# Moving the load of one weight block (the z1 half of w_in) from SyncE's DMA queue to ScalarE's in the start-up of a fused gMLP and linear-attention kernel

## Chip, cores and metric

One core of one Trainium2 chip. Times are device microseconds (us) of one execution. A run of a kernel is profiled once and timed several times in turn with the kernel before on the same chip. Engines: PE is TensorE, PEld its weight loads, ACT ScalarE, DVE VectorE, POOL GpSimd, SP SyncE; "SPq" and "ACTq" are issues of DMAs by those two. All times of single events are counted from the start of the span.

## The reference, cut to what matters

```python
# x: 2048 x 512 (bf16).  F = 1376, Fh = 688
z  = gelu(x @ w_in)                       # w_in: 512 x 1376
z1 = z[:, :Fh]                            # block "z1" of w_in
z2 = layernorm(z[:, Fh:])                 # block "z2" of w_in
b  = (z1 * (w_sp @ z2 + b_sp[:, None])) @ w_out
a  = linear_attention(x, wqkv, w_phi) @ wo
g  = sigmoid((x * gate_w).sum(-1, keepdims=True))
out = g * a + (1 - g) * b
```

The change touches only how the z1 block of `w_in` (512 x 688, 688 KB) reaches the chip.

## The kernel before: the parts that the argument needs

```python
nc.sync.dma_start(out=xs[:, 0, :], in_=x2[0:P, :])           # x tiles 0 and 1, plain
nc.scalar.dma_start(out=xs[:, 1, :], in_=x2[P:2 * P, :])
load_z2w(nc.sync, 0); load_z2w(nc.scalar, 1); load_z2w(nc.sync, 2)   # z2 block by depth slice
nc.scalar.dma_start(out=gaterow[0:NDT, :], ...)
load_z2w(nc.scalar, 3)
# ... cut: first GELU table load on ScalarE
x_dma_T(2)                                # x tiles 2, 3: transposed by the DMA
x_dma_T(3)
for h in range(2):                        # the z1 block in two halves (L136)
    nc.sync.dma_start(
        out=w_z1[:, 2 * h:2 * h + 2, :], in_=w_in_v[:, 2 * h:2 * h + 2, 0:FH])
for i in range(4, 8):
    x_dma_T(i)
# ... cut: x tiles 8 to 15, bias, wqk (transposed), eight small w_phi loads, wv, w_sp (transposed)
```

PE and ACT keep the order in which the program is written. PE first transposes x tiles 0 and 1, then computes z2 for tiles 0 to 3, then z1 for tiles 0 to 3 (`z1_tile`: four depth slices, two matmuls each, so the fifth matmul is the first to read the second half), then z2 for tiles 4 to 7, and so on. ACT applies GELU to each tile as it takes it out of PSUM (the "evictions", L203 for z2, L257 for z1).

```python
for c in range(NCH):
    ts = list(range(c * 4, c * 4 + 4))
    for tt in ts:
        if c > 0:
            z2_tile(tt)
        # ... cut
    for tt in ts:
        z1_tile(tt)
        # ... cut
```

The softmax here doesn't subtract the row's maximum and nothing guards it: scores larger than these inputs give would overflow.

## Time and profile before

| | before |
|---|---|
| time, median of the first three runs | 206.46 us (206.36 to 206.66) |
| span of the profiled run | 204.29 us, its time 206.0 |
| PE busy | 98% |
| z1 half 0: issued, landed | 4.93, 8.84 |
| z1 half 1: issued, landed | 5.57, 9.91 |
| PE's gap before the fifth matmul of z1 tile 0 | 0.26 us |

How to read it: the chain of waits names what held PE up before 10 us; the timelines of SP and ACT show when the issues left. The timeline of ACT is a good gauge of PE's gaps: ACT's evictions follow PE at 1.17 us a tile, and a longer step is a gap on PE. The last z2 and the first z1 eviction of the kernel before (start, length, engine, line, what, in brackets ACT's idle time before it):

```profile
9.31 0.74 ACT L203 ACTIVATE z2all<-zp 128x688 bf16<-128x688 f32 x1 [0.43 <-PE zp L188]
10.74 0.74 ACT L257 ACTIVATE z1all<-zp 128x688 bf16<-128x688 f32 x1 [0.68 <-PE zp L188]
```

The step is 1.43, which is 0.26 above 1.17. The span minus 10.74 is 193.55 us; that number returns below.

### The profile page before, as it was taken

How to read it: one execution, taken by the hardware profiler on the slowest of the kernel's cores; microseconds unless marked ns; L12 is line 12 of the kernel's file. 1: busy time of each engine (PE TensorE's matmuls, PEld its weight loads, DVE VectorE, ACT ScalarE, POOL GpSimd, SP SyncE). 2: the span in 40 equal slices, each digit the busy share in tenths (PEclk: the TensorE clock that was granted, in tenths of full speed). 3: DMA queues.
4: the chain of work that ended last, by engine and by line, in shares of the span. 5: the costliest groups of instructions: out<-in, count | busy, mean ns of one | idle time of the engine just before them, and what ended most of it. 6: DMA issues, size and time to landing. Idle time of an engine off the chain costs nothing.

```text
span 204.3 us, 3996 instructions
## 1 busy us (share of the span) xinstructions
PE 200.5 (98%) x1557; PEld 119.7 (59%) x1557; DVE 130.4 (64%) x283; ACT 74.6 (37%) x122; POOL 45.6 (22%) x76
## 2 busy tenths in 40 slices
PE   8999999999999999999999999999999999999994
PEld 4666666655665555656565666555555555665642
DVE  4558484838977597979797789555566645633332
ACT  3556677795222333342424042222351136002303
POOL 3020202022523325424242442222204220200000
PEclk9999999999999999999999999999999999999999
DMA  6999399999999027941322229763667458552943
GB/s 200 232 176 153 65 207 232 219 290 231 259 240 232 3 39 158 311 94 21 70 52 41 51 39 115 141 130 59 110 160 80 90 114 183 64 96 51 139 81 104
DMA packets 89947, 27.22 MB, mean 133 GB/s; under 512 B 84200, under 2 KB 89928, under 8 KB 89928
## 3 DMA queue, kind: packets, MB, share of 16 engines
q1 hardware_dynamic: 87616, 24.81, 63.5%
q10 hardware_dynamic: 2312, 2.16, 3.8%
q8 instruction: 12, 0.20, 0.4%
q14 instruction: 7, 0.06, 0.1%
HBM read 4.15 MB, written 2.10 MB: 31 GB/s over the span
## 4 chain that ended last, share of the span: by engine, by line
PE 94%; DMA 4%; SPq 1%; DVE 0%; issue 0%
PE mm L451 37%; PE zp L188 16%; PE mm L352 14%; PE mm L512 9%; PE mm L506 7%; PE mm L392 7%; DMA w_z<-in_B_w_in_dram 2%; PE kvacc L408 2%; PE at L464 2%; DMA xs<-in_A_x_dram 1%; PE mm L517 1%; SPq L131 1%; PE zp L304 0%; SPq L136 0%; PE at L475 0%; PE pq L304 0%
## 5 line engine op out<-in xcount | busy, mean ns | idle before, releaser
L451 PE MATMUL mm<-z2all,wspT 128*128 128x344 bf16 x512 | 79.9, 309 | 0.0
L451 PEld LDWEIGHTS <-wspT 128*128 128x128 bf16 x512 | 49.0, 98 | 25.3
L188 PE MATMUL zp<-w_z,xT 128*128 128x344 bf16 (+1 forms) x254 | 38.1, 309 | 0.1
L356 ACT ACTIVATE eq<-mm 128x512 bf16<-128x512 f32 x32 | 17.4, 595 | 51.4 <-PE mm L352 25.7
L360 DVE TENSOR_REDUCE zs<-eq 128x64 f32<-128x1024 bf16 x16 | 19.5, 1220 | 20.1 <-ACT eq L356 20.1
L188 PEld LDWEIGHTS <-xT 128*128 128x128 bf16 x254 | 24.5, 98 | 12.1 <-issue 0.3
L356 ACT ACTIVATE ek<-mm 128x512 bf16<-128x512 f32 x32 | 17.3, 601 | 27.1 <-PE mm L352 27.1
L456 DVE SCALAR_TENSOR_TENSOR ucat<-mm,bT,z1all 128x344 bf16<-128x344 f32 x32 | 17.4, 544 | 15.1 <-PE mm L451 15.1
L369 POOL TENSOR_TENSOR eq<-eq,ratio 128x512 bf16<-128x512 bf16 x16 | 16.9, 1055 | 44.6 <-DVE ratio L368 36.7
L528 ACT ACTIVATE ob<-mm,g_inv 128x512 bf16<-128x512 f32 (+1 forms) x15 | 10.1, 680 | 33.1 <-PE mm L517 28.5
L360 DVE TENSOR_REDUCE zs<-ek 128x64 f32<-128x1024 bf16 x16 | 19.2, 1208 | 2.8 <-ACT ek L356 2.8
L512 PE MATMUL mm<-wspT,uT 128*128 128x512 bf16 (+2 forms) x85 | 20.1, 367 | 0.0
L352 PEld LDWEIGHTS <-xT 128*128 128x128 bf16 x128 | 12.2, 98 | 12.0
L369 POOL TENSOR_TENSOR ek<-ek,ratio 128x512 bf16<-128x512 bf16 x16 | 16.9, 1055 | 2.2 <-DVE ratio L368 1.7
L506 PE MATMUL mm<-wspT,oT 128*128 128x512 bf16 (+2 forms) x68 | 16.6, 366 | 0.0
L352 PE MATMUL mm<-wq_p,xT 128*128 128x512 bf16 x64 | 16.4, 379 | 0.0
L392 PE MATMUL mm<-wv_sb,xT 128*128 128x512 bf16 x64 | 16.4, 379 | 0.0
L352 PE MATMUL mm<-wk_p,xT 128*128 128x512 bf16 x64 | 16.3, 379 | 0.0
L206 DVE BATCH_NORM_STATS2 bn<-z2all 128x6 f32<-128x344 bf16 x32 | 14.9, 502 | 0.0
L203 ACT ACTIVATE z2all<-zp 128x688 bf16<-128x688 f32 x16 | 11.8, 743 | 7.1 <-PE zp L188 7.0
L257 ACT ACTIVATE z1all<-zp 128x688 bf16<-128x688 f32 x16 | 11.9, 743 | 5.3 <-PE zp L188 4.9
L512 PEld LDWEIGHTS <-uT 128*128 128x128 bf16 x85 | 8.1, 98 | 9.4 <-issue 0.2
(77 smaller groups left out, 142.0 us busy)
## 6 DMA issues: line engine op xcount, KB each, us to landing
out_dram<-ob ACTq DMA_DIRECT2D x12, 128.0 KB, 2.6
wspT<-in_B_w_out_dram SPq DMA_DIRECT2D x2, 640.0 KB, 5.2
w_z<-in_B_w_in_dram SPq DMA_DIRECT2D x2, 344.0 KB, 4.1
wv_sb<-in_A_wqkv_dram SPq DMA_DIRECT2D x1, 512.0 KB
wspT<-in_A_wo_dram SPq DMA_DIRECT2D x2, 256.0 KB, 4.1
out_dram<-ob SPq DMA_DIRECT2D x3, 128.0 KB, 1.8
w_z<-in_B_w_in_dram ACTq DMA_DIRECT2D x2, 172.0 KB, 3.3
w_z<-in_B_w_in_dram SPq DMA_DIRECT2D x2, 172.0 KB, 3.1
```

The costliest lines, as they stand in the source:

```text
L188: nc.tensor.matmul(zp[:, j, 0:n], lhsT=xT[:, dt, tt * P:(tt + 1) * P], rhs=wt[:, dt, j * HF:j * HF + n], start=(dt == 0), stop=(dt == NDT ...
L206: nc.vector.bn_stats(out=bn6[:, tt, j, :], in_=z2v[:, j, :])
L257: nc.scalar.activation(out=z1all[:, tt, :].rearrange("p (j n) -> p j n", j=2), in_=zp[:, :, 0:HF], func=AF.Gelu_apprx_tanh,)
L352: nc.tensor.matmul(ps[:, :], lhsT=xT[:, dt, tt * P:(tt + 1) * P], rhs=w[:, dt, :], start=(dt == 0), stop=(dt == NDT - 1))
L356: nc.scalar.activation(out=e[:, :, a, :], in_=ps[:, :].rearrange("p (h f) -> p h f", f=DH), func=AF.Exp, scale=1.0 - 2.0 * a)
L360: nc.vector.tensor_reduce(out=z[:].rearrange("p h a -> p (h a)"), in_=e[:].rearrange("p h a f -> p (h a) f"), axis=AX.X, op=ALU.add,)
L369: nc.gpsimd.tensor_tensor(out=e[:, :, 1, :], in0=e[:, :, 1, :], in1=ratio[:, :, None].to_broadcast([P, H, DH]), op=ALU.mult)
L392: nc.tensor.matmul(v_ps[:, :], lhsT=xT[:, dt, tt * P:(tt + 1) * P], rhs=wv_sb[:, dt, :], start=(dt == 0), stop=(dt == NDT - 1))
L451: nc.tensor.matmul(gp[:, 0:HF], lhsT=wspT[:, st, tt * P:(tt + 1) * P], rhs=z2all[:, st, j * HF:(j + 1) * HF], start=(st == 0), stop=(st == ...
L456: nc.vector.scalar_tensor_tensor(out=ucat[tt % NU][:, c0 + j * HF:c0 + (j + 1) * HF], in0=gp[:, 0:HF], scalar=bT[:, tt:tt + 1], in1=z1all[ ...
L506: nc.tensor.matmul(acc, lhsT=oTs[tt][:, g, :], rhs=wo_t[:, g, c0:c1], start=start and g == 0, stop=stop and g == NG - 1)
L512: nc.tensor.matmul(acc, lhsT=uTs[tt][:, i + ft, :], rhs=w_main[i][:, ft, c0:c1], start=start and ft == 0, stop=False)
```

## The change

Intent: ACT is idle between its copy of x tile 1 and its first eviction. If it issues the two z1 halves there, SP's queue holds transposed x tiles alone, these can be issued 1.1 us earlier, and the z1 block no longer stands behind x tiles 2 and 3.

```diff
-    for h in range(2):
-        nc.sync.dma_start(
-            out=w_z1[:, 2 * h:2 * h + 2, :], in_=w_in_v[:, 2 * h:2 * h + 2, 0:FH])
+    def load_z1w(eng, h):
+        eng.dma_start(out=w_z1[:, 2 * h:2 * h + 2, :], in_=w_in_v[:, 2 * h:2 * h + 2, 0:FH])
+
     for i in range(4, 8):
         x_dma_T(i)
@@
         x_T(1, 2, NDT, pq_tile([P, 2, P], BF16)[:, :, :], on_act=True)
+        for h in range(2):
+            load_z1w(nc.scalar, h)
         one(0, 0, 0)
```

## The prediction

> **What bounds the kernel now.** I read the page first (busy shares, slices, chain), then the chain in order of time over the first 30 us, then the timelines of SP and ACT there, the table by stretches, and last the waits each instruction carries in the program. The page says at once that TensorE is the bound:
>
> ```profile
> PE 200.5 (98%) x1557; PEld 119.7 (59%) x1557; DVE 130.4 (64%) x283; ACT 74.6 (37%) x122; POOL 45.6 (22%) x76
> PE   8999999999999999999999999999999999999994
> PEclk9999999999999999999999999999999999999999
> ```
>
> Between the start-up and the last output tiles PE is never idle and the granted clock is full. So any delay of PE before that is carried to the end one for one, and nothing after the start-up is there to be won. The change touches only the first 17 us. The chain in order of time there:
>
> ```profile
> 0.80 2.88 DMA xs<-in_A_x_dram
> ...
> 3.70 1.19 SPq L131
> ...
> 4.93 0.59 SPq L136
> ...
> 5.57 4.34 DMA w_z<-in_B_w_in_dram
> ...
> 9.96 13.59 PE zp L188 x92
> ```
>
> Columns are start, length, what. The second half of the z1 block is issued by SP at 5.57 and lands at 9.91, and from 9.96 PE runs without a pause: 13.59 / 92 = 148 ns per matmul. How long had PE waited? The timeline of PE and of its weight loads around it:
>
> ```profile
> 9.55 0.71 PE L188 MATMUL zp<-w_z,xT 128*128 128x344 bf16 x2
> 9.96 0.10 PEld L188 LDWEIGHTS <-xT 128*128 128x128 bf16 x1 [0.31 <-issue]
> ```
>
> The last matmul before the gap starts at 9.55, so the next was due at 9.55 + 0.148 = 9.70 and started at 9.96: a stall of 0.26 us. ScalarE shows the same, with z1 evictions 1.17 us apart but 1.43 us from the last z2 eviction to the first z1 one (9.31 to 10.74). This 0.26 us, 0.13% of the time, is all that an earlier z1 block can give. The matmul that stalls is the fifth of z1 tile 0, the first that reads the second half. The first was due at 9.55 - 3 x 0.148 = 9.11; the first half, issued at 4.93 with 3.9 us to landing, was there at 8.83.
>
> The issuing engines (timelines of SP and ACT):
>
> ```profile
> 2.20 2.69 SPq L131 DMA_TRANSPOSE xT<-in_A_x_dram  x2
> 4.93 1.10 SPq L136 DMA_DIRECT2D w_z<-in_B_w_in_dram  x2
> 6.08 5.13 SPq L131 DMA_TRANSPOSE xT<-in_A_x_dram  x4
> ...
> 4.47 0.37 ACT L280 COPY xT<-pq 128x256 bf16<-128x256 bf16 x1 [0.22 <-PE pq L277]
> 6.68 2.21 ACT L203 ACTIVATE z2all<-zp 128x688 bf16<-128x688 f32 x3 [1.84 <-PE zp L188]
> ```
>
> SP is occupied all through: some 1.2 to 1.3 us for each transposed x tile, 1.10 us for the two halves of z1. ACT has an opening of 1.84 us between its copy and the first z2 eviction. That opening is what the change aims at.
>
> **What the Trainium skill says.** The page "DMA: Bandwidth & Descriptors", section "Issuing engines are not separate DMA queues", says that transfers from scalar, sync and gpsimd end up on the same 16 engines and interleave, so that a second issuing engine saves only issue time. Its section "Queues, rings and completion order" says that each DMA engine takes turns between the queues, a packet at a time. The z1 block therefore leaves the SP queue, but then shares the engines with the x transposes that used to stand behind it. The trace of before has one queue active there: from 7 to 9 us SP's queue alone fills the engines (90.7% and 108.7% by the queue table of those microseconds) at 312 and 372 GB/s, and the transposes follow. So before gives the z1 block the engines alone; sharing in this stretch is not shown yet. The same page, section "Anatomy of one DMA — SWDGE (gpsimd) path", says that DMA engines never wait on semaphores; the issuing sequencer does, before it dispatches. The trace agrees: the transpose of x tile 3 is issued at 3.70, 0.02 after x landed at 3.68. The page "Perfetto Trace Analysis", section "DMA Instruction — HWDGE (DVE, Sync)", says that the descriptor generator is locked for exclusive use by one issue. The trace speaks against a long lock: ACT issues its last z2 weight load at 2.35 in 0.37 us, while SP's first x transpose, from 2.20 for 1.29 us, is under way.
>
> **The change part by part.** TensorE's, VectorE's and GpSimd's instructions keep their order; two issues move from SP to ACT, behind the copy. But their waits change. Every hardware DMA carries one of eight completion semaphores, given out in turn in program order, and an issue first waits until the earlier user of its semaphore has landed. The program's order shows it:
>
> ```
> before  SP   z1 half 0 [waits DMAHW1]   z1 half 1 [waits DMAHW2]
> after   ACT  z1 half 0 [waits DMAHW5]   z1 half 1 [waits DMAHW7]
> ```
>
> In before, 1 and 2 belong to an x tile and a z2 weight slice that had long landed. In after, PE's waits tell the owners: its first matmul of z2 depth slice 2 waits for 5, so that is SP's second z2 slice; its first matmul of x tile 2 waits for 7, so that is the transpose of x tile 2.
>
> Step 1, half 0. SP issues z2 slice 2 at about 1.7, with some 3.1 to 3.2 us to landing: 4.9. So half 0 is issued at about 4.9, as before (4.93). No gain.
>
> Step 2, half 1. The transpose of x tile 2 is issued at 2.20; the view of its stretch gives its time to landing:
>
> ```profile
> L131 SPq DMA_TRANSPOSE xT<-in_A_x_dram x1: 1285/1285/1285, 2.2 to 2.2; - x1
> DMA to landing us min/median/max: 4.0/4.0/4.0
> ```
>
> So it lands at 6.2, and half 1 is issued at 6.2, where before had 5.57: 0.65 us later.
>
> Step 3, its way to landing. Estimates from before: half 0 was issued at 4.93 and data rose at about 7.0, so some 2.0 us pass first: data from 8.2. A half is 0.35 MB and takes 1.0 us of all 16 engines (0.68 MB in 7 to 9 us). A transposed x tile is 512 packets; 1143 packets took 0.87 + 0.62 = 1.49 us of all engines in 10 to 12 us, so 0.67 us a tile. SP now issues tiles 4, 5, 6 at about 4.9, 6.2, 7.4. About one tile lies beside each half: 0.3 to 0.7 us more for each, and half 0 can push half 1. Data of half 1 thus ends between 9.5 and 10.2, and the rest to the semaphore takes about 0.5 (before: bytes used up at about 9.4, landing 9.91). Landing 10.0 to 10.7, middle 10.5.
>
> Step 4, PE. Fifth matmul of z1 tile 0 at about 10.55 in place of 9.96: the stall grows from 0.26 to about 0.85, which is +0.6 us.
>
> Step 5, what ACT pays. The sequencer is blocked until 6.2 and then issues for some 0.5 us (0.46 and 0.59 on SP), to about 6.75. The first z2 eviction moves from 6.68 to about 6.8. PE's z2 tile 3 needs that PSUM buffer at about 9.11 - 8 x 0.148 = 7.93; VectorE's read of it ended at 7.62 before, so 0.1 to 0.2 later is still in time. Cost on the path: 0.
>
> Step 6, what SP wins: x tiles 4 to 7 and all later loads are issued up to 1.1 us earlier. Tile 4 is wanted after z1 tile 3, at about 9.96 + 0.148 x 28 = 14.1, and lands in before at 6.08 + 4.3 = 10.4. Hidden anyway: 0.
>
> Sum: 206.46 + 0.6 = 207.05; I say 207.0.
>
> **The rivals.** (a) The change works as meant: the block leaves the SP queue, lands earlier, and the stall of 0.26 us goes: 206.2. For it: the x transposes no longer stand ahead of it, and z2 slices of half the size issued by ACT land in 3.3 us, so with 0.5 us for the other 172 KB half 1 could land at 6.2 + 3.8 = 10.0 if the engines were free. Even that is no earlier than 9.91, so only an earlier landing of x tile 2 could make (a) true. (b) The queues share badly, many small transpose packets holding up the large rows, and half 0 is late as well (wanted at 9.11): a landing at 11.2 or later makes 207.7 to 208.3. For it: the engines are near full from 4 us on. Against: SP's issue rate spaces the transposes 1.28 us apart for 0.67 us of work, so there is room. (c) ACT becomes the bound, if its issue lengthens under contention: one output store took 1.01 us to issue in place of 0.34. The first eviction would be at 7.3, z2 tile 3 would wait about 0.3 us, and that largely runs in front of the same landing, so it adds little: 207.1. (d) All is lost in noise: three runs of before span 0.3 us.
>
> **Range and chances.** The gain is capped at 0.26 us and the loss at perhaps 1.5 us, so 206.3 to 207.9 should hold it 8 times in 10. 2% would be 4.1 us, which none of the rivals reaches: faster 0.01, within 2% 0.98, slower 0.01.
>
> **What would show it.** Half 1's issue on ACT near 6.2, right after x tile 2's landing, with half 0 near 4.9 (steps 1, 2); half 1's landing near 10.5 (3); PE's gap before the fifth z1 matmul near 0.85, and everything later shifted by the same (4); first z2 eviction at 6.8 without a new gap on PE near 8 (5); x tile 4 issued at about 4.9 without any PE wait removed (6). I am wrong if half 1 is issued before 6 us or lands before 9.7, if PE waits for half 0, or if a gap opens after 15 us.

## The result, and the profile after

The changed kernel took 207.58 us (median of 6 runs, 206.90 to 208.22), the kernel before 206.47 (6 runs, 206.28 to 206.84). The ratio is 1.0055, 95% interval 1.0031 to 1.0080: within 2%, and slower clear of noise, by about 1.1 us. (Here and below a ratio is the mean time of one kernel's fast runs over the mean of the other's of the same rounds, so not quite the ratio of the medians.)

The chain of waits of the changed kernel (start, length, what):

```profile
2.20 4.12 DMA xT<-in_A_x_dram
6.32 0.02 issue
6.34 4.48 DMA w_z<-in_B_w_in_dram
10.82 0.04 issue
10.86 13.59 PE zp L188 x92
```

It still ends in half 1 of the z1 block (`w_z`), but half 1 now hangs on the landing of x tile 2 (`xT`): 2.20 + 4.12 = 6.32, issue at 6.34, landing at 10.82 where before had 9.91. The run of 92 matmuls behind it is the same 13.59 us.

The timelines of SP and ACT:

```profile
2.20 8.15 SPq L131 DMA_TRANSPOSE xT<-in_A_x_dram  x6
```

```profile
4.58 0.37 ACT L282 COPY xT<-pq 128x256 bf16<-128x256 bf16 x1 [0.34 <-PE pq L279]
5.28 1.44 ACTq L136 DMA_DIRECT2D w_z<-in_B_w_in_dram  x2
6.93 2.21 ACT L203 ACTIVATE z2all<-zp 128x688 bf16<-128x688 f32 x3 [1.98 <-PE zp L188]
9.57 0.74 ACT L203 ACTIVATE z2all<-zp 128x688 bf16<-128x688 f32 x1 [0.43 <-PE zp L188]
11.64 0.74 ACT L259 ACTIVATE z1all<-zp 128x688 bf16<-128x688 f32 x1 [1.33 <-PE zp L188]
```

The two issues span 1.44 us though each took 0.4: between them lies the wait for x tile 2. The step from the last z2 to the first z1 eviction is 2.07, so PE's gaps there sum to 0.90. On PE itself (timeline, PE and its weight loads):

```profile
9.77 0.46 PE L188 MATMUL zp<-w_z,xT 128*128 128x344 bf16 x2
```

```profile
10.86 7.31 PE L188 MATMUL zp<-w_z,xT 128*128 128x344 bf16 x49 [0.63 <-DMA w_z<-in_B_w_in_dram]
```

```profile
9.47 0.55 PEld L188 LDWEIGHTS <-xT 128*128 128x128 bf16 x5 [0.29 <-DMA w_z<-in_B_w_in_dram]
```

The fourth matmul of z1 tile 0 starts at 9.92 (second of the two from 9.77), the fifth was due at 10.07 and started at 10.86: a gap of 0.79. The weight load at 9.47 shows that PE also waited a little for half 0.

From the first z1 eviction on nothing differs: 205.19 - 11.64 = 193.55, as in before. The whole difference of the two profiled runs, 0.90 us, is the later first z1 eviction. This makes that eviction a clock for all that follows: in nine of the thirteen traces the rest takes 193.54 to 193.57 us. In the other four it is 193.68 to 194.61, and those are named where they come.

The profiled run was the fastest of the six (206.9). So its trace explains 0.90 us, and the mean loss of 1.1 is larger; the experiments had to find out what varies.

Where do the bytes go slower? DMA queue table of the kernel before for 7 to 8 us (queue, packets, MB, time of the packets as a share of 16 engines), then of the changed kernel for 8 to 9 us:

```profile
q1 hardware_dynamic: 235, 0.31, 90.7%
```

```profile
q10 hardware_dynamic: 97, 0.12, 77.9%
q1 hardware_dynamic: 474, 0.11, 56.3%
```

q1 is SP's queue, q10 ACT's. Before: 0.907 x 16 us / 235 = 62 ns for a packet, which is a row of the z1 block (1,376 B; 8 of the 235, and 11 of the 97 below, are packets of 4 B). After, with 474 packets of the transposes beside them: 0.779 x 16 us / 97 = 128 ns a row, and 0.12 MB in the microsecond in place of 0.31. It is the worst microsecond of that trace: the same sum gives 63 ns from 7 to 8 us and 85 from 9 to 10.

The mean also hides how the time was lost. In the packet records of all thirteen traces (packets of 1,376 B that start between 6 and 12.5 us) the median z1 row takes 59 to 61 ns. What differs is how many of the 512 rows took over 200 ns: 18 in before, 54 in after. So most rows go as fast as ever, and some stall.

### The profile page after: what moved, and what is told of

Read it like the earlier page. It is cut to its first block, busy times and chain, and to the rows that moved or that the text cites. A ratio compares the mean times of both kernels' runs of the same rounds, so it can differ in the third digit from the quotient of the medians.

```text
span 205.2 us, 3977 instructions
## 1 busy us (share of the span) xinstructions
PE 199.8 (97%) x1539; PEld 119.4 (58%) x1557; DVE 130.4 (64%) x283; ACT 74.6 (36%) x122; POOL 45.8 (22%) x76
## 4 chain that ended last, share of the span: by engine, by line
PE 93%; DMA 4%; issue 1%; SPq 1%; DVE 0%
PE mm L453 36%; PE zp L188 16%; PE mm L354 13%; PE mm L514 8%; PE mm L394 7%; PE mm L508 7%; DMA w_z<-in_B_w_in_dram 2%; DMA xT<-in_A_x_dram 2%; PE kvacc L410 2%; PE at L466 2%; PE mm L519 1%; SPq L117 0%; PE zp L306 0%; PE at L477 0%; SPq L119 0%
## 5 line engine op out<-in xcount | busy, mean ns | idle before, releaser
L508 PE MATMUL mm<-wspT,oT 128*128 128x512 bf16 (+2 forms) x61 | 15.6, 364 | 0.4
```

The lines of the kernel that those rows point to most:

```text
L508: nc.tensor.matmul(acc, lhsT=oTs[tt][:, g, :], rhs=wo_t[:, g, c0:c1], start=start and g == 0, stop=stop and g == NG - 1)
```

## The experiments

Two causes offer themselves. **Theory A, late issue:** the semaphore that half 1 drew makes it wait for x tile 2, 0.6 to 0.8 us later than before. **Theory B, sharing:** the z1 rows now run beside the transposes of x tiles 4 to 7, which in before stood behind them in the same queue (the last rows had company there too: 194 packets under 512 B from 8.5 to 9 us). They can be separated, since one can force the order in which the completion semaphores are given out (a dependency that only orders) and can make one DMA wait for another's landing (a real dependency). Eleven runs follow, with four to six timed runs each (rep_before one); the edits are shown against the changed kernel, the kernel before or the experiment that they build on, and are shortened. In the table, "step" is the time from the last z2 to the first z1 eviction minus 1.17, that is PE's gaps at the start of z1; all but the ratio is from the traces.

| run | ratio to before (95%) | half 1 issued, landed, took | step | first z2, first z1 eviction |
|---|---|---|---|---|
| before | 1 | 5.57, 9.91, 4.34 | 0.26 | 6.68, 10.74 |
| rep_before | one look | 5.46, 9.55, 4.09 | 0 | 7.26, 11.06 |
| after | 1.0055 (1.0031 to 1.0080) | 6.34, 10.82, 4.48 | 0.90 | 6.93, 11.64 |
| rep_after | 1.0031 (1.0012 to 1.0050) | 6.12, 10.04, 3.92 | 0.15 | 6.90, 10.86 |
| late_free | 1.0082 (1.0057 to 1.0107) | 6.63, 12.16, 5.53 | 1.59 | 7.59, 12.99 |
| early_free | 1.0042 (1.0012 to 1.0073) | 5.60, 10.00, 4.40 | 0 | 8.03, 11.83 |
| early_free_2 | 1.0047 (1.0025 to 1.0069) | 4.99, 10.96, 5.97 | 0.42 | 7.57, 11.79 |
| early_held | 1.0073 (1.0034 to 1.0111) | 4.99, 9.26, 4.27 | 0 | 7.34, 11.14 |
| late_held | 1.0120 (1.0075 to 1.0166) | 7.27, 10.38, 3.11 | 0 | 7.70, 11.95 |
| late_sp | 1.0026 (1.0011 to 1.0041) | 6.70, 10.05, 3.34 | 0 | 7.14, 10.94 |
| fill_held | 1.0010 (0.9996 to 1.0023) | 4.99, 9.64, 4.64 | 0 | 7.74, 11.54 |
| fill_late | 1.0023 (1.0008 to 1.0038) | 6.37, 10.05, 3.69 | 0 | 7.34, 11.14 |
| split3 | 1.0006 (0.9993 to 1.0019) | in two parts, last 9.47 | 0 | 7.42, 11.22 |

The first four experiments ran on one chip (before there: 205.65 to 207.20), the other seven on another (205.88 to 206.54). One of late_held's six runs (211.52) was slow and is left out. One each of early_held (209.86) and late_held (210.46) counts, though its granted clock was 0.992; by the medians of the rest over that of before, 206.40, these two ratios would be 1.0047 and 1.0083.

### early_free: early semaphores, transposes free

All further SP loads are written behind the z1 halves and ordered after them without a wait:

```diff
-        for h in range(2):
-            load_z1w(nc.scalar, h)
+        load_z1w(nc.scalar, 0)
+        half1 = load_z1w(nc.scalar, 1)
+        rest_loads(half1, NoSync)      # x tile 4 ordered after half1, no wait; the rest in program order
```

> The changed kernel, but the z1 halves get completion semaphores 1 and 2, whose earlier users (two loads that landed before 5 us) are long done; the x transposes of SP run on freely beside them. Theory A, late issue: the cost comes from half 1 waiting at ScalarE for x tile 2 (6.3 us). Then half 1 is issued by 5.5 us, lands by 10.1, PE's gap before the fifth z1 matmul is 0.3 us or less, and the time is 206.2 to 206.7, like before. Theory B, sharing: the cost comes from the x transposes on the other queue. Then half 1 still needs 5 us or more to landing, PE waits 0.7 us or more, and the time stays at 207.2 or above.

Measured: 1.0042. Half 1 landed at 10.00 and there was no gap at z1, as A has it, and yet the time was not that of before. The trace shows a late start of PE instead: the small gate row (1 KB, issued at 1.75) landed only at 5.94. Timeline of PE:

```profile
5.99 0.18 PE L300 MATMUL pq<-ident,gaterow 128*128 128x4 bf16 x1 [0.57 <-DMA gaterow<-in_gate_w_dram]
```

In before this matmul started at 4.64. Neither theory had said this, so a third was put up, **theory C**: a z1 block issued by ACT as early as 4.57 takes turns from the z2 slices and x tiles 2 and 3, which PE needs first. In this trace half 1 was not early either: the z2 slice that had used its semaphore before landed at 5.58, not before 5 us as expected. By the way, 4.57 is where ACT's copy of x tile 1 starts (4.56 to 4.93), not where it ends: the issue did not wait for the copy, only for its place in ACT's order.

### early_held: early semaphores, transposes held

```diff
-        rest_loads(half1, NoSync)
+        rest_loads(half1, Sync)        # x tile 4 waits for the landing of half 1
```

> As early_free, and SP's transpose of x tile 4 (with all behind it) waits until half 1 has landed, so the z1 block has the DMA engines alone after x tile 3. Theory A: as early_free within 0.2 us, 206.2 to 206.6. Theory B: clearly below early_free, by 0.5 us or more, at 206.2. Under both, half 1 should land 3.6 to 4.2 us after its issue, before 9.7, so that PE's gap there is gone; x tile 4 is then issued at about 9.7 and lands at 13.7 to 14.1, just before PE wants it at about 14.1, so a new gap of up to 0.3 us may open there.

Measured: 1.0073. At z1 it did what B says: half 1 landed at 9.26, no gap. DMA queue table for 7 to 8 us:

```profile
q10 hardware_dynamic: 292, 0.38, 105.1%
```

1.051 x 16 us / 292 = 58 ns a row, alone on the engines, as before. The time is worse all the same, because all later loads moved by 3 us and a new wait came where both theories had looked at x tile 4 only: at the fold of w_k (PE multiplies w_k by w_phi once, for the attention part) PE waits for w_phi. Waits of PE's weight loads between 12 and 60 us:

```profile
PEld L317 <- DMA wphi<-in_A_w_phi_dram: 0.7, 1, 0.7
```

The rest after the first z1 eviction is 194.37 us, 0.82 more than elsewhere. So the run says nothing on B by its time; it had to be repeated without this side effect (fill_held).

### late_held: half 1 late on ACT, transposes held

```diff
+        follow(half1, x_tile_2, Sync)  # half 1 waits for the landing of x tile 2
         rest_loads(half1, Sync)
```

> Semaphores as in early_held and SP held as there, but half 1 is made to wait for the landing of x tile 2, as in the changed kernel. Theory A: half 1 issued at 6.3, landing at 10.0 to 10.5 even with the engines to itself, PE's gap 0.4 to 0.8 us; together with x tile 4 held until then (landing near 14.3, wanted near 14.7) 206.6 to 207.1. Theory B: without sharing the landing is early enough, 206.2 to 206.5.

Measured: 1.0120. Half 1 alone on the engines took only 3.11 us, the shortest of all. But x tiles 2 and 3 themselves landed late, with half 0 issued at 4.35 beside them. The chain of waits:

```profile
3.54 5.82 DMA xT<-in_A_x_dram
9.36 0.05 issue
9.40 14.63 PE zp L198 x99
```

x tile 3 took 5.82 us from issue to landing, where before had 6.78 - 3.70 = 3.08, and PE stood still for it. That half 0 did this is argued, not shown: in the six runs that issued it at 4.56 or 4.57, x tile 3 took 3.18 to 4.04 us. The fold waited for w_phi here too (rest 194.61). The time decides nothing between A and B.

### late_free: half 1 late on ACT, transposes free

```diff
+        follow(half1, x_tile_2, Sync)
         rest_loads(half1, NoSync)
```

> Half 1 made to wait for x tile 2, transposes free: the changed kernel rebuilt from the parts of the three others, apart from the semaphore of half 0. Theories A and B: 206.9 to 208.2, like the changed kernel. If it is at 206.5 instead, then neither the late half 1 nor the sharing is the cause but the wait of half 0 (issued at 5.28 in the changed kernel, 4.93 in the one before).

Measured: 1.0082. This is the changed kernel again in all that matters, with half 0 drawing another semaphore and issued at 4.57 in place of 5.28. It shows how bad sharing can be: the view of the issue gives 5.5 us to landing, and the next eviction comes 2.76 us after the last (timeline of ACT):

```profile
L137 ACTq DMA_DIRECT2D w_z<-in_B_w_in_dram x1: 402/402/402, 6.6 to 6.6; - x1
DMA to landing us min/median/max: 5.5/5.5/5.5
```

```profile
10.23 0.74 ACT L213 ACTIVATE z2all<-zp 128x688 bf16<-128x688 f32 x1 [0.42 <-PE zp L198]
12.99 0.74 ACT L271 ACTIVATE z1all<-zp 128x688 bf16<-128x688 f32 x1 [2.02 <-PE zp L198]
```

### rep_before: the kernel before, a second trace

No edit.

> The kernel before once more, for a second trace of its start-up. If the landings of the start-up hardly scatter, the third z2 slice lands at 4.9 to 5.1, x tiles 2 and 3 at 6.1 to 6.4 and 6.7 to 7.0, the z1 halves at 8.8 and 9.9, PE's gap before the fifth z1 matmul is 0.2 to 0.4 us, and the time is 206.1 to 206.9. Theory C (a z1 block issued by ScalarE at 4.6 takes turns from the z2 slices and from x tiles 2 and 3, which PE needs first) needs these earlier here than in the four runs so far that issued it there: 5.84 to 6.15, 6.55 to 7.19 and 7.17 to 9.36. If they are as late here, that was the chip and not the kernel.

Measured: 206.31 us, and theory C lost its evidence. In this kernel the z1 block stands behind x tile 3 in the one queue, and yet the third z2 slice landed at 5.94, x tiles 2 and 3 at 6.55 and 7.04, about as late as in the four runs above (all but late_held's x tiles). The landings of the start-up scatter by up to a microsecond by themselves. PE's first z2 matmuls were slower too: 0.45 us each here, 0.31 in the first trace, at a clock row of 1.00 in both. A small effect of C is not excluded: the first z2 eviction comes at 7.34 to 8.03 in all seven traces that issue half 0 by 4.57, at 6.68 to 7.42 in the other six. But six of those seven, and two of the other six, also have the slow first matmuls, which were slow from about 3.9 us on, before any z1 issue; and fill_held below, which issues both halves as early, costs 0.10%, not clear of zero. The timeline of ACT:

```profile
7.26 2.21 ACT L203 ACTIVATE z2all<-zp 128x688 bf16<-128x688 f32 x3 [2.33 <-PE zp L188]
9.89 0.74 ACT L203 ACTIVATE z2all<-zp 128x688 bf16<-128x688 f32 x1 [0.43 <-PE zp L188]
11.06 0.74 ACT L257 ACTIVATE z1all<-zp 128x688 bf16<-128x688 f32 x1 [0.42 <-PE zp L188]
```

PE started 0.6 us late, found half 1 there (9.55), had no gap at z1, and ended 0.3 us later than in the first trace. So PE's own start and half 1's landing run side by side, and the later of the two counts. A late start of PE hides a late half 1, and that is why one trace of a kernel can mislead here.

### rep_after: the changed kernel, a second trace

No edit.

> The changed kernel once more, on the chip of the others of this call. Ratio 1.003 to 1.008. Half 1 is issued right after the landing of x tile 2, at 6.2 to 6.6, and takes 4.4 to 5.6 us to landing because the transposes are beside it; PE's gap before the fifth z1 matmul 0.7 to 1.8 us.

Measured: 1.0031, at the low end of the expected range; half 1 issued at 6.12, with 3.92 us to landing, below the expected range. Its profiled run was again the fastest of its six (206.12, of 206.12 to 207.57), so this trace too shows a lucky case, with a gap of only 0.15 (0.7 to 1.8 was expected). Its span, 204.41, is even below the 204.60 of rep_before, though the timed runs put the kernel 0.31% above. Of its z1 rows 14 took over 200 ns, against 54 in the first trace.

### early_free_2: early_free once more

> early_free again, since its profile had PE start late (the gate row landed at 5.94 us) and no gap at z1. Theory C: the time stays 0.5 to 1.2 us above before, with no gap at z1 and the loss before it: the first z2 eviction at 7.2 or later, where before has 6.68. If that late start was chance, the first eviction is at 6.7 to 6.9 and the time is 206.2 to 206.7.

Measured: 1.0047. The late start of the first trace was chance: here the third z2 slice landed at 5.17, x tiles 2 and 3 at 6.21 and 6.71. The first z2 eviction is at 7.57, but with no wait for a DMA before it: the first z2 matmuls ran at 0.45 us as in rep_before. And this time the loss is at z1, with an early half 1. The chain of waits:

```profile
4.99 5.97 DMA w_z<-in_B_w_in_dram
10.96 0.04 issue
11.00 13.01 PE zp L198 x88
```

Half 1 was issued at 4.99, earlier than in any run with the wait, and landed at 10.96, later than in the changed kernel's own traces. Theory A alone cannot make that. DMA queue table for 8 to 9 us:

```profile
q10 hardware_dynamic: 72, 0.10, 96.3%
q1 hardware_dynamic: 89, 0.02, 18.2%
```

The engines show as full, yet little gets through: at 62 ns a row and 21 ns a transpose packet (0.745 x 32 us / 1,143, the packets that the prediction counts from 10 to 12 us), this work alone would take (72 x 62 + 89 x 21) ns / 16 = 0.40 us, an estimate from before. In this trace 66 z1 rows took over 200 ns. Two runs of this kernel on two chips give 0.42 and 0.47%.

### late_sp: the kernel before, half 1 late, in the one queue

```diff
+    # half 1, still on SP, waits for the landing of x tile 2
+    tc.add_manual_dep(half.ins, x_tile_2.ins.name, Sync)
```

> The kernel before, both z1 halves on SP as there, but half 1 made to wait for the landing of x tile 2 as in the changed kernel (one 4 KB load of the bias is issued in the pause). It is late without sharing: the transposes stay behind it in the one queue. Theory A (late issue is the cost): half 1 issued at 6.2 to 6.6, landing at 10.4 or later, time 206.8 or above, ratio 1.003 or more. Theory B (sharing is the cost): it lands within 3.2 to 3.8 us, at 9.6 to 10.2, because it now meets empty engines, so PE's gap stays at 0.5 us or less; ratio 1.000 to 1.0015.

Measured: 1.0026 (1.0011 to 1.0041), between the two theories' numbers. Landing as B expected:

```profile
L137 SPq DMA_DIRECT2D w_z<-in_B_w_in_dram x1: 388/388/388, 6.7 to 6.7; - x1
DMA to landing us min/median/max: 3.3/3.3/3.3
```

Issued at 6.70, 1.13 us later than before, it landed at 10.05, only 0.14 later: a half that meets empty engines makes up most of its lateness. In the trace PE itself was late (it had waited for the third z2 slice until 5.98), so the loss of the timed runs, 0.0026 x 206.2 = 0.5 us, is not seen in it. The timed runs put it on this edit, which makes half 1 late and also moves x tile 4 and the loads behind it by 1.1 us (7.14 in place of 6.08). That the lateness is what costs is argued.

### fill_held: sharing removed, without the side effect

```diff
     def rest_loads(h1, how):
+        brow load, five of the eight w_phi loads      # SP's pause is filled with small loads
         follow(x_tile_4, h1, Sync)                    # x tile 4 waits for half 1
         ...
-        brow load, eight w_phi loads
+        the other three w_phi loads
```

> z1 on ScalarE with the early semaphores, x tiles 4 and on held until half 1 has landed as in early_held, but SP uses the pause for the bias and five of the eight small w_phi loads, so that the loads behind come only about 0.5 us late and the fold of w_k should not wait for them. Theory B: half 1 lands at 9.0 to 9.8, no gap before z1 above 0.1 us and no gap at the fold: ratio 0.999 to 1.001, the 0.3 to 0.5% of the runs with sharing gone. Theory A does not distinguish it from early_free (1.004).

Measured: 1.0010 (0.9996 to 1.0023), not to be told from the kernel before, and its interval does not meet that of early_free_2 on the same chip. z1 on ACT, early, without transposes beside it, costs nothing that these rounds can see. It gains nothing either. The trace has no gap at z1 or at the fold (rest 193.54).

### fill_late: the same, with half 1 late

> fill_held with half 1 made to wait for x tile 2: late on ScalarE, without sharing except with half 0. Theory B: half 1 issued at 6.2 to 7.0, lands within 3.1 to 3.8 us at 9.6 to 10.5, PE's gap 0 to 0.7 us, ratio 1.000 to 1.003, below late_free (1.0082). Theory A: ratio 1.005 or more, as the changed kernel.

Measured: 1.0023 (1.0008 to 1.0038), like late_sp, by quite another path. Half 1 took 3.69 us. This run has a control for what sharing means, since SP sends small w_phi packets while ACT's rows are under way. DMA queue table for 8 to 9 us:

```profile
q10 hardware_dynamic: 193, 0.25, 76.6%
q1 hardware_dynamic: 145, 0.00, 8.0%
```

0.766 x 16 us / 193 = 64 ns a row, though 145 packets of the other queue went beside it. So a second queue as such did not slow the rows. Nor do transposes on it always. DMA queue table of early_free for 7 to 8 us:

```profile
q10 hardware_dynamic: 168, 0.21, 60.6%
q1 hardware_dynamic: 377, 0.10, 42.4%
```

0.606 x 16 us / 168 = 58 ns a row beside 377 packets of the transposes; the changed kernel's 128 beside 474 is one case, not a price per packet. (The rest is 193.76 us here: a weight load of PE waited 0.4 us for an x tile later. So about 0.2 us, 0.1%, of this trace's loss is not at z1, and the ratio is not clear of that of fill_held.)

### split3: half 1 in two loads, all on SP

```diff
-    for h in range(2):
-        nc.sync.dma_start(out=w_z1[:, 2 * h:2 * h + 2, :], ...)
+    for d0, d1 in ((0, 2), (2, 3), (3, 4)):
+        nc.sync.dma_start(out=w_z1[:, d0:d1, :], ...)
```

> The kernel before with its second z1 half issued as two loads of one depth slice each, all by SP, so that PE's fifth z1 matmul waits for half as many bytes. Slice 2 issued near 5.5 should land near 9.4 to 9.6, before PE wants it at 9.70, slice 3 near 9.9 to 10.1, wanted at about 10.0. Gap of 0.26 us gone or down to 0.1; time 206.2 to 206.5, ratio 0.998 to 1.000, at the edge of what the rounds can tell.

Measured: 1.0006 (0.9993 to 1.0019), the same. The slices landed at 8.91 and 9.47, before PE wanted them, but PE started late in this trace (first z2 eviction 7.42), so nothing was there to be saved. (The rest is 193.68 us.) The 0.26 us of the first trace of before is not there in every run: rep_before has no gap at all. No version beats the kernel before.

## Why the prediction was right or wrong

The direction, the size class and the chain were right: half 1 waits on ACT for x tile 2, lands later, and PE's gap before the fifth z1 matmul grows. The time, 207.0, was below the measured median of 207.58 in the first rounds and close to that of rep_after (206.88, which is 0.7 above the kernel before there, 206.20; 0.6 was predicted). That the second comes so near is in part chance, since the six timed runs of the changed kernel spread over 1.3 and 1.5 us in the two calls. Step by step:

1. Half 0 at about 4.9. The gate was named rightly (third z2 slice), but that landing scatters from 4.96 to 6.15 over the traces: half 0 was issued at 5.28 and 5.05. It landed at 9.43 in the first trace, and PE did wait for it, which the prediction had put down as a sign of being wrong. It cost nothing, because half 1 was later still.
2. Half 1 at 6.2: 6.34 and 6.12. Right.
3. **The way to landing is the term that holds only in part.** Predicted about 4.3 us (6.2 to 10.5), from adding the work of one transposed tile beside each half. In the changed kernel's two traces it measured 4.48 and 3.92, so there the sum came out; but both are the fastest of their six runs. Beside free transposes in the other kernels it was 5.53, 4.40 and 5.97. At like distance between the two issues: 0.42 us apart, 5.97 free against 4.27 and 4.64 held; about 1.9 us apart, 5.53 free (late_free) against 3.34 and 3.69. Adding busy times fits some microseconds (after, 8 to 9 us: (97 x 62 + 474 x 21) ns / 16 = 1.0 us) and fails in others (early_free_2: 0.40 us of work filled one). What it has no term for is the stalled rows: 32 to 66 rows took over 200 ns in after, late_free, early_free_2 and late_held, which are the four traces with the longest gaps of PE for a z1 half or x tile in the start-up (0.42 to 1.59 us), and 1 to 19 in the other nine. A loose reading besides: before did not give the z1 block the engines alone to its end, since small packets ran beside its last rows from 8.5 us.
4. The gap: 0.79 in place of 0.85 in the first trace, 0.15 in the second, and from late_free's 12.16 about 1.6 in a bad case. The prediction also took PE to be ready at 9.70, as in the one trace at hand; in the second trace of the same kernel it was 0.6 us later. Two quantities that scatter, the later of which counts, were treated as two fixed ones.
5. ACT's cost on the path: none, right. The first eviction came at 6.93 in place of 6.8, but ACT was waiting for PE there, not for its own issue, and PE had no gap before z2 tile 3.
6. SP's earlier issues: hidden, right. x tile 4 was issued at 5.15, 0.9 us earlier, and the rest after the first z1 eviction is 193.55 us in both kernels.

On the shares of the two causes: with half 1 late but no transposes beside it the loss is 0.26 and 0.23% (late_sp, fill_late), with the transposes beside it but no wait for x tile 2 0.42 and 0.47% (early_free twice), with neither 0.10%, not clear of zero (fill_held), and with both 0.31 to 0.82% (after, rep_after, late_free). What is shown is that letting the transposes run beside an early z1 block costs time, and that holding them back removes it (early_free_2 against fill_held, one chip, intervals apart). How the changed kernel's own loss divides is not shown: on that chip rep_after, with both, lost 0.31%, no more than early_free_2, so the two do not add, and the intervals of late_sp, fill_late, rep_after and early_free_2 overlap. The prediction saw both causes, but gave most of the 0.6 us to late issue; that sharing is as large fits the point values. Rival (a), that the change works as meant, needed more than the lost semaphore: early_free had that and was no faster. Rival (b), bad sharing with a landing after 11.2, is what late_free showed (12.16; its profiled run took 208.24). That such landings raise the changed kernel's mean above the prediction is likely, but its slower runs were not traced.

Open stays what stalls the rows, and why the time of half 1 beside transposes varies between 3.9 and 6.0 us. That the engines' turns between the queues do it could be argued from the Trainium skill's "DMA: Bandwidth & Descriptors", section "Queues, rings and completion order", which says that an engine takes turns between queues packet by packet; no run shows the turns, and the median row, 59 to 61 ns with and without transposes, gives no sign of them.

## What to carry to other kernels

A load moved to an idle issuing engine leaves its place in a queue, and that place can be what protected it: here most of the z1 rows had the engines to themselves because the transposes stood behind them. Before moving an issue, look at which earlier DMA its completion semaphore belongs to, and at what will be in flight beside it, transposes above all. In a start-up where two scattered times race, judge by several rounds and several traces, and use one late event with a constant rest behind it (here the first z1 eviction plus 193.55 us) to tell where a difference arose.

## What the Trainium skill lacked or had wrong

- "DMA: Bandwidth & Descriptors", section "Rules for kernel authors", says that spreading DMAs over several issuing engines does not help bandwidth and only saves issue time, and that a transpose next to ordinary DMAs "needs nothing". As a rule of correctness no run here contradicts the second. What the page lacks is that it can cost time: with the transposes beside the early z1 block this kernel lost 0.42 and 0.47%, and 0.10%, not clear of zero, with them held back. Rows of 1,376 B took 58 and 128 ns on average in two microseconds with 377 and 474 transpose packets from the other queue beside them, 62 in one queue, 58 alone and 64 beside small plain copies. The median was 59 to 61 ns throughout; what raises the mean is single rows of over 200 ns.
- None of the pages cited here says that a DMA's issue may wait for an unrelated one because both use the same completion semaphore in turn (the traces show eight, and this program gives them out). Here that moved an issue from 5.57 to 6.34 us, though no data depended on it.
- "Perfetto Trace Analysis", section "DMA Instruction — HWDGE (DVE, Sync)", speaks of an exclusive lock of the descriptor generator. In the two traces of the changed kernel ACT's z1 issues took 0.38 to 0.41 us though they overlap SP's issues of transposes, 1.2 to 1.3 us each, so no long lock shows. (Elsewhere one took 0.58 us beside a transpose in early_free_2, and 0.62 with none being issued in early_held.)
- "TensorE: Matmul & The Clock Gate", section "What's actually happening", says that the warm-up ends at a point that varies from run to run. The traces fit that: the first z2 matmuls took 0.31 us in one trace of the kernel before and 0.45 in another. The clock row of the profile read 1.00 in both, so it does not show the warm-up, if that is what it was. The page does warn of the trace's clock records in general; what it lacks is this case of a row that reads full speed.
